# Attention of a sink-and-window layer: float32 probabilities and values in packed column halves instead of float32r high and low parts

## The chip, the cores and the metric

The kernel runs on one core of a Trainium2 chip. The metric is the time of one execution in device microseconds (us); three runs of the kernel before gave 791.02, 791.50 and 791.93, so its time is 791.5 us (median).

## What is computed

Attention over 4 batches, 8 heads, 768 positions, head size 64. Each query sees the last 128 positions up to its own and the first 4 positions (the "sinks"). The output of all heads is the input of a gated feed-forward layer (called MoE in the code) with float64 weights that reach the core as pairs of 32-bit words.

```python
scores = scale * np.matmul(q, k.transpose(0, 1, 3, 2))
keep = is_sink | in_window            # 4 sinks, window of 128
a = np.exp(scores - max); a = a / (sum(a) + 1e-09)
x = np.matmul(a, v)                   # -> 3072 x 512
out = ((x @ w_a) * (x @ w_b)) @ w_out # 512 -> 1536 -> 512
```

## The kernel before, in words

**Chunks.** The rows are worked in eight chunks (CHUNKS, L221): batch, first block of 128 positions, number of blocks nt. The first is (0, 0, 4), the second (0, 4, 2), the other six have nt = 3, three of them from block 0 and three from block 3. While TensorE runs the feed-forward part of chunk c (`moe`, L755), the attention of chunk c + 1 is given out in small steps between its groups of matmuls (`between`, L878). The attention of the first chunk stands alone at the start. The feed-forward part of the last chunk stands alone at the end. In time: about 0 to 52 us the first attention; 52 to 170 the MoE of chunk 0 with the attention of chunk 1 in it, and with the decoding of the weights from words to float32r on VectorE and ScalarE (`weight_bits` to `weight_low`, L324 to L353); then MoE of chunk 1 with the attention of chunk 2 (from block 0), to about 232; then MoE of chunks 2 to 6 with the attention of chunks 3 to 7 (from blocks 0, 3, 3, 0, 3), to about 700.

**The pipeline.** `pipeline` (L713) walks over units (head h, block i). Step k gives out the scores of unit k, then, three units behind, the product with the values of a head whose last unit has been turned (`av`), then the sink products, then the transposes of the unit two behind. This is the order in which the program names the work. The order in which each engine's queue gets it is fixed by a planner before the run, from its own costs and due times; an engine works its queue in order and waits on semaphores.

**Exact attention** (`parts_exact`, L587) serves chunk 0 and the heads 0 to 3 of chunk 1. Scores, probabilities, values and products are float32. The probabilities of a unit are turned by one or two transposes on TensorE (L668) and copied by ScalarE (L669) into a tile that holds two heads. `av` (L671) works on odd heads only: for each block of keys it issues one matmul for the even head into PSUM partitions 0 to 63 (64 columns of the array) and one for the odd head into partitions 64 to 127 (L684). One copy (L687) of 128 partitions brings both heads to `xf`.

**Split attention** (`parts_split`, L456) serves everything else: the heads 4 to 7 of chunk 1 and all heads of chunks 2 to 7, 52 heads in all. Every operand of a matmul is a float32r high part and a float32r rest.
- `prep_v` (L409) loads the values of two heads into an "io" tile (a ring of six), and for each head rounds them (L382 on GpSimd) and takes the rest (L385), so that one 128-column weight tile `vv` holds both parts. In chunk 1 ScalarE (L380) and VectorE (L385) do this.
- The scores are two matmuls (L485, `s`). For late blocks (t >= 2) of batches 1 to 3 the two halves of the window are joined on VectorE by L491 into one square ("joined" units), then follow L493, exp on ScalarE (L495), L497 and L498 on VectorE, and two scalings on ScalarE, L503 for the probabilities `p` and L504 for the sinks `sc`.
- `transposes` of a joined unit: one transpose on TensorE (L524) into a slot of the PSUM tile `t`; ScalarE rounds it (L527); VectorE spreads it by a triangle mask to the two slots of the high part (L528); ScalarE rounds it again into `p` (L530); VectorE subtracts in place (L531) and spreads the rest (L532). Other units: two transposes (L539), a rounding copy (L542), a subtraction (L543).
- `av` of every head multiplies high and low parts (L555): five matmuls of 256 columns where the chunk starts at block 0, seven (five of 256 columns, two of 128) where it starts at block 3, six in chunk 1. The high and low products of the values lie in opposite partition halves, so a copy (L560), an addition (L561) and for nt = 3 another addition (L563) put them together.

Of the kernel before, what the change touches and what calls it, by code (L numbers as in the profile page):

```python
# [7 lines left out]
F32 = mybir.dt.float32  # L8
BF16 = mybir.dt.bfloat16
F32R = mybir.dt.float32r  # L10
# [3 lines left out]
ALU = mybir.AluOpType  # L14
# [3 lines left out]
B, H, S, D = 4, 8, 768, 64  # L18
DM, FF = 512, 1536
P = 128  # L20
# [4 lines left out]
NS = 8  # L25
KB = P + NS
KC = NB * P + (NB - 1) * NS
SW = 2 * P + NS
MB = 4
# [50 lines left out]
def general_path(tc, ident, val, kT, qT, vB, wa, wb, wo, out):  # L80
# [130 lines left out]

UNITS = {3: ((0, 4, "BA"), (1, 2, "AB"), (3, 5, "AB")), 2: ((0, 4, "BA"), (1, 5, "AB"))}
GROUPS = {
    3: ((0, 0, 2, 0), (1, 2, 2, 1), (2, 5, 0, 2), (-1, 4, 1, 0)),
    2: ((0, 0, 2, 0), (1, 5, 1, 1), (-1, 4, 1, 0)),
}


CHUNKS = ((0, 0, 4), (0, 4, 2), (1, 0, 3), (2, 0, 3), (1, 3, 3), (2, 3, 3), (3, 0, 3), (3, 3, 3))  # L221


class Fast:
# [184 lines left out]
    def prep_v(self, b, h, t0, nt):  # L409
        s0, nb, kw, u = self.geometry(b, h, t0, nt)  # L410
        if h % 2 == 0:
            self.vr = self.io([P, 2, MB, D], F32, f"vr{u}")
            self.nc.sync.dma_start(self.vr[:, :, :nb], self.vB[b, h // 2, :, :, s0:s0 + nb])
        vr = self.vr[:, h % 2, :nb]
        vv = self.sp.tile([P, MB, P], F32R, tag="vv", name=f"vv{u}")
        kh, kl = self.halves(h)
        self.round(vv[:, :nb, kh], vr)
        self.rest(vv[:, :nb, kl], vr, vv[:, :nb, kh])
        if h % 4 == 0 and t0 + nt > 2:
            vsr = self.io([P, 2, P], F32, f"vsr{u}")  # L420
# [5 lines left out]
        return vv  # L426

    def attention(self, b, t0, nt, xf, exact=False, alone=False, heads=range(H), bank=None):

# [26 lines left out]
    def parts_split(self, b, t0, nt, xf, alone, heads, bank):  # L456
        nc = self.nc
        tag = f"{b}_{t0}"
        s0 = max(t0 - 1, 0)
        late = [i for i in range(nt) if t0 + i >= 2]  # L460
        units = [(h, i) for h in heads for i in range(nt)]
        tps, preps, state, sc, vss, avs, skt = {}, {}, {}, {}, {}, {}, {}
        banks = self.banks
        joined = late if b else []

        def product(name):
            if bank is None:
                return self.ps.tile([P, 4 * P], F32, tag="av", name=name)
            return self.half_bank(bank, 1, name).rearrange("p c q -> p (c q)")

        def do_prep(h):
            if h in heads:
# [37 lines left out]
        def transposes(h, i):  # L510
            p = state.pop((h, i))
            t = t0 + i
            u = f"{tag}_{h}_{i}"
            n = units.index((h, i))
            if bank is not None:
                tp = self.half_bank(bank, 0, f"t{u}")
            else:
                k = n % len(banks)
                if k not in tps:
                    tps[k] = self.ps.tile([P, 4, P], F32, tag=banks[k], name=f"t{u}")  # L520
                tp = tps[k][:, 2 * (n % 2):2 * (n % 2) + 2, :]
            c1, c2, order = UNITS[nt][i]
            if i in joined:
                nc.tensor.transpose(tp[:, 0, :], p[:, NS:KB], self.ident)  # L524
                hs, ls = (self.pt_split()[:, part, c1:c2 + 1:c2 - c1, :] for part in range(2))
                tri = self.tri if order == "AB" else self.tri[:, ::-1]
# [7 lines left out]
            parts = {"A": p[:, :P], "B": p[:, P + NS:]}  # L534
            if t == 0:
                parts["B"] = p[:, :P]
                order = "B"
            for k, o in enumerate(order):
                nc.tensor.transpose(tp[:, k, :], parts[o], self.ident)  # L539
            n = len(order)  # L540
            hs, ls = (self.pt_split()[:, part, c1:c1 + (n - 1) * (c2 - c1) + 1:c2 - c1, :] for part in range(2))
            nc.scalar.copy(hs, tp[:, :n, :])  # L542
            nc.vector.tensor_tensor(ls, tp[:, :n, :], hs.bitcast(F32), op=ALU.subtract)  # L543

        def av(h):
            vv = preps[h][3]
            ps = product(f"av{tag}_{h}")
            pt = self.pt_split()
            products = []
            for k, sl, ns, c in GROUPS[nt]:  # L550
                if t0 + k >= 0:
                    moving = [pt[:, part, sl:sl + ns, :] for part in range(2)] if ns else [pt[:, :, sl, :]]
                    products += [(t0 + k - s0, m, slice(c * P, (c + (ns or 2)) * P)) for m in moving]
# [3 lines left out]
            x = xf[h // 2]  # L557
            n = nt * P
            mn, mi = self.halves(h)
# [18 lines left out]
        def sinks_av(g, pr):  # L578
            n = len(late) * P
            ps = product(f"sk{tag}_{g}_{pr}")  # L580
            nc.tensor.matmul(ps[:, :n], lhsT=vss[g][:, pr, :], rhs=skt[g][:, :n], start=True, stop=True)
            xs = xf[2 * g + pr][:, late[0] * P:nt * P]
            nc.vector.tensor_tensor(xs, ps[:, :n], xs, op=ALU.add)

        return do_prep, scores, transposes, av, sinks_t, sinks_av

    def parts_exact(self, b, t0, nt, xf, alone, heads, bank):  # L587

        nc = self.nc
        tag = f"{b}_{t0}"  # L590
        s0 = max(t0 - 1, 0)
        nb = t0 + nt - s0
        kw = nb * KB - NS
        late = [i for i in range(nt) if t0 + i >= 2]
        units = [(h, i) for h in heads for i in range(nt)]
        preps, state, sc, vss, pts, skt = {}, {}, {}, {}, {}, {}

        def do_prep(h):
            if h not in heads:
# [54 lines left out]
        def transposes(h, i):  # L654
            p = state.pop((h, i))
            t = t0 + i
            u = f"{tag}_{h}_{i}"
            if not pts:
                pts[0] = self.cp.tile([P, 2, 7, P], F32, tag="pt", name=f"ptx{u}")
# [9 lines left out]
            nc.scalar.copy(pts[0][:, h % 2, k:k + len(parts), :], tp[:, :len(parts), :])  # L669

        def av(h):  # L671
            if h % 2 == 0:
                return
            v = preps[h][2]
            if alone:
                ps = self.ps.tile([P, 4, P], F32, tag="av", name=f"av{tag}_{h}")
            else:
                ps = self.half_bank(bank, 1, f"av{tag}_{h}")
            pin = self.tc.keep_in_program_order
            for blk in range(nb):  # L680
                i0, i1 = max(s0 + blk - t0, 0), min(s0 + blk - t0 + 2, nt)
                sl = 2 * (s0 + blk - t0) + (t0 > 0) + (i0 > s0 + blk - t0)
                for e in range(2):
                    pin(nc.tensor.matmul(ps[e * D:(e + 1) * D, i0:i1, :], lhsT=v[:, e, blk, :],  # L684
                                         rhs=pts[0][:, e, sl:sl + i1 - i0, :], start=blk == 0, stop=blk == nb - 1,
                                         skip_group_check=True))
# [291 lines left out]
```

## Time and profile before

| what | value |
|---|---|
| median of three runs | 791.5 us |
| the profiled execution | 790.77 us |
| its span, first to last instruction | 789.1 us |
| TensorE matmul (PE) busy | 768.3 us, 97% |
| VectorE (DVE) busy | 515.3 us, 65% |
| ScalarE (ACT) busy | 475.5 us, 60% |
| GpSimd (POOL) busy | 290.0 us, 37% |
| mean granted TensorE clock | 0.994 of full speed |

PE is the matmul row and PEld the weight loads, which overlap with it. A matmul's printed duration runs from its start until its result is out. The next one starts before that, so durations of neighbours overlap, and the time that a matmul adds is read from the step between the ends of two neighbours. The chain of waits prints its pieces with just these steps.

### The profile page before, as it was taken

What the parts mean: (1) busy time and instruction counts of PE and PEld (TensorE: products, weight loads), DVE (VectorE), ACT (ScalarE), POOL (GpSimd) and SP (SyncE); (2) the same over time, 40 slices, a digit from 0 to 9 for tenths busy, and PEclk for the clock granted to TensorE, in tenths of its full rate; (3) what the DMA queues carried; (4) which work ended last, traced back from release to release, by engine and by line L of the source; (5) the groups of instructions that cost most, each with busy time, mean ns of one, the idle gap of its engine ahead of it and who ended that gap; (6) DMA issues with size and microseconds to landing.
All of it is one profiled execution on the core that took longest, in us unless ns stands there. A gap on an engine that the chain in (4) does not pass through costs nothing.

```text
span 789.1 us, 13664 instructions
## 1 busy us (share of the span) xinstructions
PE 768.3 (97%) x4293; PEld 673.3 (85%) x4293; DVE 515.3 (65%) x1759; ACT 475.5 (60%) x1479; POOL 290.0 (37%) x400
## 2 busy tenths in 40 slices
PE   8879999999999999999999999999999999999997
PEld 4558777779899999998899889899999988989996
DVE  6878999977774675367763777636765478643321
ACT  5876667747755776466663766547774566644431
POOL 1100000246642664265651756416545466101110
PEclk9989999999999999999999999999999999999999
DMA  8987100142221342412111111113333112005511
GB/s 318 345 310 294 60 18 10 65 142 58 59 68 41 107 132 79 138 31 62 55 48 50 47 43 49 57 41 98 111 119 102 58 52 63 28 30 183 175 55 42
DMA packets 44572, 75.82 MB, mean 96 GB/s; under 512 B 4592, under 2 KB 24016, under 8 KB 44496
## 3 DMA queue, kind: packets, MB, share of 16 engines
q1 hardware_dynamic: 41440, 69.40, 27.0%
q10 hardware_dynamic: 3024, 5.51, 1.9%
q8 instruction: 35, 0.57, 0.3%
q14 instruction: 41, 0.34, 0.1%
q0 software_dynamic: 32, 0.00, 0.0%
HBM read 68.60 MB, written 6.29 MB: 95 GB/s over the span
## 4 chain that ended last, share of the span: by engine, by line
PE 84%; DVE 9%; ACT 3%; DMA 1%; issue 1%; SPq 0%; DVEq 0%; ACTq 0%; POOLq 0%
PE b L769 23%; PE a L769 23%; PE o L778 22%; PE s L485 4%; PE av L555 4%; PE t L524 2%; PE s L631 2%; PE t L539 1%; DVE g L794 1%; DMA kx<-in_kD_dram 1%; PE av L684 1%; DVE w L353 1%; PE t L668 1%; ACT p L495 1%; DVE gl L799 1%
## 5 line engine op out<-in xcount | busy, mean ns | idle before, releaser
L769 PE MATMUL a<-xh,w 128*128 128x384 f32 (+2 forms) x768 | 216.6, 342 | 2.2 <-ACT g L788 1.3
L769 PE MATMUL b<-xh,w 128*128 128x384 f32 (+2 forms) x768 | 214.1, 340 | 0.0
L778 PE MATMUL o<-w,gh 128*128 128x512 f32 x576 | 186.6, 402 | 0.2 <-ACT gh L797 0.2
L769 PEld LDWEIGHTS a<-xh,w 128*128 128x128 f32 x768 | 138.9, 188 | 7.7 <-ACT g L788 1.7
L769 PEld LDWEIGHTS b<-xh,w 128*128 128x128 f32 x768 | 138.8, 188 | 3.7
L799 POOL TENSOR_TENSOR gl<-g,gh 128x384 fp32r<-128x384 f32 x60 | 61.0, 1017 | 188.2 <-ACT gh L797 185.9
L769 PE MATMUL a<-xl,w 128*128 128x384 f32 (+2 forms) x384 | 130.0, 339 | 0.0
L769 PE MATMUL b<-xl,w 128*128 128x384 f32 (+2 forms) x384 | 130.0, 338 | 0.0
L794 DVE TENSOR_TENSOR g<-b,g 128x384 f32<-128x384 f32 (+2 forms) x96 | 53.1, 554 | 108.0 <-PE b L769 97.5
L778 PEld LDWEIGHTS o<-w,gh 128*128 128x128 f32 x576 | 104.2, 189 | 18.5 <-ACT gh L797 0.8
L778 PE MATMUL o<-w,gl 128*128 128x512 f32 x288 | 114.8, 399 | 0.4 <-DVE gl L799 0.4
L788 ACT COPY g<-a 128x384 f32<-128x384 f32 (+2 forms) x96 | 45.5, 474 | 72.6 <-PE a L769 66.7
L797 ACT CAST gh<-g 128x384 fp32r<-128x384 f32 (+2 forms) x96 | 49.1, 512 | 64.1 <-DVE g L794 61.6
L769 PEld LDWEIGHTS a<-xl,w 128*128 128x128 f32 x384 | 72.6, 189 | 2.8 <-issue 0.3
L769 PEld LDWEIGHTS b<-xl,w 128*128 128x128 f32 x384 | 72.5, 189 | 2.2 <-issue 0.3
L495 ACT ACTIVATE p<-p,st 128x264 f32<-128x264 f32 (+1 forms) x152 | 65.4, 430 | 13.6 <-DVE st L493 12.1
L382 POOL TENSOR_SCALAR ks<-kr 64x400 fp32r<-64x400 f32 (+1 forms) x48 | 28.8, 600 | 108.0 <-DVE pt L543 105.9
L778 PEld LDWEIGHTS o<-w,gl 128*128 128x128 f32 x288 | 54.3, 188 | 13.2 <-DVE gl L799 1.7
L382 POOL TENSOR_SCALAR qh<-qr 128x384 fp32r<-128x384 f32 x48 | 25.1, 522 | 103.7 <-PE s L485 96.5
L385 POOL TENSOR_TENSOR ks<-kr,ks 64x400 fp32r<-64x400 f32 (+1 forms) x48 | 57.9, 1205 | 3.9
L503 ACT ACTIVATE p<-p,st 128x128 f32<-128x128 f32 x96 | 38.6, 402 | 24.4 <-DVE st L498 21.8
L555 PE MATMUL av<-pt,vv 128*128 128x256 f32 (+1 forms) x288 | 50.3, 285 | 0.2 <-DVE pt L532 0.2
(153 smaller groups left out, 1388.8 us busy)
## 6 DMA issues: line engine op xcount, KB each, us to landing
qr<-in_qT_dram SPq DMA_DIRECT2D x48, 192.0 KB, 2.4
raw<-in_wa_dram SPq DMA_DIRECT2D x12, 512.0 KB, 6.3
raw<-in_wb_dram SPq DMA_DIRECT2D x12, 512.0 KB, 6.2
raw<-in_wo_dram SPq DMA_DIRECT2D x12, 512.0 KB, 6.0
chk_a<-in_wa_dram SPq DMA_DIRECT2D x24, 256.0 KB, 2.9
chk_b<-in_wb_dram SPq DMA_DIRECT2D x24, 256.0 KB, 2.9
chk_o<-in_wo_dram SPq DMA_DIRECT2D x24, 256.0 KB, 2.8
out_dram<-os ACTq DMA_DIRECT2D x21, 256.0 KB, 2.1
```

Of the source, the lines that this page charges most:

```text
L382: self.nc.gpsimd.tensor_scalar(o, i, 1.0, 1.0, op0=ALU.mult, op1=ALU.mult)
L385: (self.nc.vector if self.no_gpsimd else self.nc.gpsimd).tensor_tensor(o, i, high.bitcast(F32), op=ALU.subtract)
L485: nc.tensor.matmul(ps[:, :w], lhsT=q[:, i * P:(i + 1) * P], rhs=ks[:, c0:c0 + w], start=m == 0, stop=m == 1)
L495: nc.scalar.activation(p[:, :w], p[:, :w], AF.Exp, bias=st[:, 0:1], scale=-1.0, accum_out=st[:, 1:2])
L503: nc.scalar.mul(p[:, NS:KB], p[:, NS:KB], st[:, 3:4])
L555: nc.tensor.matmul(ps[:, cols], lhsT=vv[:, blk, :], rhs=m, start=n == 0, stop=n == len(products) - 1, skip_group_check=True)
L769: nc.tensor.matmul(ps[:, :n], lhsT=w[:, ksl], rhs=x[:, :n], start=kk == 0 and i == 0, stop=kk == NK - 1 and i == 2)
L778: nc.tensor.matmul(outs[i], lhsT=g[:, sl], rhs=w, start=j == 0 and k == 0, stop=j == NJ - 1 and k == 2)
L788: nc.scalar.copy(g[:, :n], pa[:, :n])
L794: nc.vector.tensor_tensor(g[:, :n], pb[:, :n], g[:, :n], op=ALU.mult)
L797: nc.scalar.copy(gh[:, :n], g[:, :n])
L799: e.tensor_tensor(gl[:, :n], g[:, :n], gh[:, :n].bitcast(F32), op=ALU.subtract)
```

## The change

All attention keeps probabilities and values in float32 and uses the product in column halves of the exact attention, for odd heads only, into one PSUM tile. A new function `values` holds that product, for both kinds of attention; it goes through the blocks of keys from the last to the first, and in each takes the odd head first. In split attention, scores, the feed-forward part and the sink products stay as they are. The values of two heads go from memory straight into a "vv" tile (a ring of two). L380, L382 and L385 are gone for the values. Of a joined unit the transpose and one masked multiplication remain; of the others the transposes and the copy. L560, L561 and L563 become one copy of 128 partitions for two heads.

```diff
-    def pt_split(self):
+    def turned(self):
...
-            self.pt = self.cp.tile([P, 2, 7, P], F32R, tag="pt", name="pt")
+            self.pt = self.cp.tile([P, 2, 7, P], F32, name="pt")
...
     def prep_v(self, b, h, t0, nt):
...
-            self.vr = self.io([P, 2, MB, D], F32, f"vr{u}")
-            self.nc.sync.dma_start(self.vr[:, :, :nb], self.vB[b, h // 2, :, :, s0:s0 + nb])
-        vr = self.vr[:, h % 2, :nb]
-        vv = self.sp.tile([P, MB, P], F32R, tag="vv", name=f"vv{u}")
-        kh, kl = self.halves(h)
-        self.round(vv[:, :nb, kh], vr)
-        self.rest(vv[:, :nb, kl], vr, vv[:, :nb, kh])
+            self.v = self.sp.tile([P, 2, MB, D], F32, tag="vv", name=f"v{u}")
+            self.nc.sync.dma_start(self.v[:, :, :nb], self.vB[b, h // 2, :, :, s0:s0 + nb])
...
+    def values(self, ps, v, t0, nt):
+        s0 = max(t0 - 1, 0)
+        nb = t0 + nt - s0
+        pt = self.turned()
+        for blk in reversed(range(nb)):
+            i = s0 + blk - t0
+            i0, i1 = max(i, 0), min(i + 2, nt)
+            sl = 2 * i + (t0 > 0) + (i < 0)
+            for e in (1, 0):
+                self.tc.keep_in_program_order(self.nc.tensor.matmul(
+                    ps[e * D:(e + 1) * D, i0:i1, :], lhsT=v[:, e, blk, :], rhs=pt[:, e, sl:sl + i1 - i0, :],
+                    start=blk == nb - 1, stop=blk == 0, skip_group_check=True))
...
             if i in joined:
                 nc.tensor.transpose(tp[:, 0, :], p[:, NS:KB], self.ident)
-                nc.scalar.copy(tp[:, 1, :].bitcast(F32R), tp[:, 0, :])
-                nc.vector.tensor_tensor(hs, tp[:, 1:2, :].broadcast_to([P, 2, P]), tri, op=ALU.mult)
-                hj = p[:, NS:KB].bitcast(F32R)
-                nc.scalar.copy(hj, tp[:, 0, :])
-                nc.vector.tensor_tensor(tp[:, 0, :], tp[:, 0, :], hj.bitcast(F32), op=ALU.subtract)
-                nc.vector.tensor_tensor(ls, tp[:, 0:1, :].broadcast_to([P, 2, P]), tri, op=ALU.mult)
+                nc.vector.tensor_tensor(pt[:, k:k + 2, :], tp[:, 0:1, :].broadcast_to([P, 2, P]), self.tri,
+                                        op=ALU.mult)
                 return
...
-            nc.scalar.copy(hs, tp[:, :n, :])
-            nc.vector.tensor_tensor(ls, tp[:, :n, :], hs.bitcast(F32), op=ALU.subtract)
+            nc.scalar.copy(pt[:, k:k + len(parts), :], tp[:, :len(parts), :])

         def av(h):
...
-            for n, (blk, m, cols) in enumerate(products):
-                nc.tensor.matmul(ps[:, cols], lhsT=vv[:, blk, :], rhs=m,
-                                 start=n == 0, stop=n == len(products) - 1, skip_group_check=True)
...
-            nc.scalar.copy(x[mn, :n], ps[mi, :n])
-            nc.vector.tensor_tensor(x[mn, :n], ps[mn, :n], x[mn, :n], op=ALU.add)
-            if nt > 2:
-                nc.vector.tensor_tensor(x[mn, 2 * P:], ps[mn, 3 * P:], x[mn, 2 * P:], op=ALU.add)
+            if h % 2 == 0:
+                return
+            ps = product(f"av{tag}_{h}")
+            self.values(ps, preps[h][3], t0, nt)
+            nc.scalar.copy(xf[h // 2][:, :nt * P].rearrange("p (c q) -> p c q", q=P), ps[:, :nt, :])
```

In `parts_exact` the same `turned` tile and the same `values` take the place of its own (the loop over blocks went from the first to the last there, the even head first).

## Rows read from the trace of the kernel before

**Rows 1.** The page: busy time of the engines over the whole span, and the chain of work that ended last, by engine.

```profile
PE 768.3 (97%) x4293; PEld 673.3 (85%) x4293; DVE 515.3 (65%) x1759; ACT 475.5 (60%) x1479; POOL 290.0 (37%) x400
PE 84%; DVE 9%; ACT 3%; DMA 1%; issue 1%; SPq 0%; DVEq 0%; ACTq 0%; POOLq 0%
```

**Rows 2.** Four rows on three stages: the busy time of DVE from 104 to 180 us (stretch, its length, DVE busy and instructions, granted clock, DMA share, GB/s), and the chain of waits by line of the stretches 104 to 180 us, 256 to 330 us and 330 to 427 us, in this order.

```profile
104.00:180.00 76.00, 67.81 (x150) 1.00 0.19 61
by line: PE a L769 14.0%; PE o L778 13.6%; PE b L769 13.3%; DVE w L353 8.4%; DVE wf L343 6.2%; DVE wf L336 6.1%; PE s L485 3.6%; DVE gl L799 3.6%; DVE xl L751 3.6%; issue 3.4%; DVE g L794 3.4%; DVE wf L334 3.1%; DVE pt L543 2.2%; DVE p L493
by line: PE o L778 28.4%; PE b L769 28.3%; PE a L769 25.3%; PE av L555 6.8%; PE s L485 5.7%; PE t L539 3.7%; PE t L524 1.1%; PE sk L581 0.6%; PE skt L570 0.3%; issue 0.0%
by line: PE b L769 25.9%; PE a L769 24.4%; PE o L778 22.9%; PE s L485 5.5%; PE av L555 4.8%; PE t L524 4.1%; DVE g L794 2.3%; DVE pt L532 1.3%; issue 1.2%; ACT gh L797 1.1%; ACT xf L560 1.0%; PE sk L581 0.9%; DVE pt L528 0.9%; PE skt L570 0
```

**Rows 3.** Groups of instructions by line over the whole span: line, engine, operation, tiles, count | busy us, mean ns of one | idle time of the engine just before them and what ended it.

```profile
L531 DVE TENSOR_TENSOR t<-t,p 128x128 f32<-128x128 f32 x96 | 28.5, 297 | 8.8 <-ACT p L530 6.9
L532 DVE TENSOR_TENSOR pt<-t,tri 128x256 fp32r<-128x256 f32 x96 | 40.5, 422 | 1.5
L561 DVE TENSOR_TENSOR xf<-av,xf 64x384 f32<-64x384 f32 x48 | 26.6, 555 | 24.3 <-ACT xf L560 23.3
L527 ACT CAST t<-t 128x128 fp32r<-128x128 f32 x96 | 24.4, 254 | 18.8 <-PE t L524 18.4
L530 ACT CAST p<-t 128x128 fp32r<-128x128 f32 x96 | 25.1, 261 | 16.9 <-DVE pt L528 15.2
L385 POOL TENSOR_TENSOR vv<-vr,vv 128x192 fp32r<-128x192 f32 (+1 forms) x48 | 32.7, 681 | 3.1
```

**Rows 4.** The product with the values before (L555). The first row is from the chain of waits in a stage from block 0: start, time added, piece, number of matmuls. The next two are the timeline of PE in a stage from block 3: start, time until the last result is out, matmuls. The last three are from the chain of waits of another head of that stage.

```profile
255.88 0.60 PE av L555 x5
...
366.24 0.28 PE L485 MATMUL s<-ks,ql 128*128 128x264 f32 x1
366.36 0.93 PE L555 MATMUL av<-pt,vv 128*128 128x256 f32 x7
...
346.94 0.24 PE av L555 x2
348.40 0.15 PE av L555
349.54 0.41 PE av L555 x4
```

**Rows 5.** The product in column halves (L684) of the exact heads, amid the MoE matmuls of chunk 0. The first four rows are the chain of waits from 93.5 to 97 us, the fifth that of the stretch inside the group alone; the sixth gives the weight loads of such groups (minimum, median, maximum ns, then first and last start). One product of the program shows as two matmuls here, since it is full float32.

```profile
93.29 0.93 PE o L778 x4
94.22 0.45 PE s L631 x2
94.66 1.02 PE t L684 x12
95.68 0.90 PE a L769 x3
...
94.92 0.65 PE t L684 x8
...
L684 PEld LDWEIGHTS t<-ptx,vx x24: 133/137/137, 94.6 to 116.0; 128*64 128x64 f32 x24
```

**Rows 6.** Groups by line again (columns as in rows 3): the transposes of joined units, the products before, the turned sinks and the sink product of chunk 1. The idle time of PEld is that before a weight load, that of PE before a matmul.

```profile
L524 PEld LDWEIGHTS t<-ident,p 128*128 128x128 f32 x96 | 13.4, 140 | 10.7 <-issue 6.3 <-ACT sc L504 3.3 <-ACT g L788 0.5
L524 PE MATMUL t<-ident,p 128*128 128x128 f32 x96 | 27.5, 287 | 2.1 <-DVE pt L532 1.9
L555 PEld LDWEIGHTS av<-pt,vv 128*128 128x128 f32 x288 | 41.4, 189 | 5.2 <-DVE pt L532 1.9 <-issue 1.1
L555 PE MATMUL av<-pt,vv 128*128 128x256 f32 (+1 forms) x288 | 50.3, 285 | 0.2 <-DVE pt L532 0.2
L570 PEld LDWEIGHTS skt<-ident,sc 128*32 128x32 f32 x26 | 2.3, 95 | 2.4 <-PE av L555 1.1 <-PE o L778 0.8 <-issue 0.4
L581 PE MATMUL t<-sct,vs 128*128 128x256 f32 x2 | 0.7, 374 | 1.6 <-DVE xf L561 1.6
L581 PEld LDWEIGHTS t<-sct,vs 128*128 128x128 f32 x2 | 0.4, 186 | 2.3 <-ACT raw L335 2.0 <-DVE xf L583 0.3
```

**Rows 7.** The timeline of a few us in a stage from block 3, all engines (start, us, engine, line; in brackets the idle time before it and what ended it).

```profile
361.56 0.42 DVE L532 TENSOR_TENSOR pt<-t,tri 128x256 fp32r<-128x256 f32 x1
...
362.10 0.14 PEld L524 LDWEIGHTS t<-ident,p 128*128 128x128 f32 x1 [0.75 <-issue]
...
362.13 0.30 PE L524 MATMUL t<-ident,p 128*128 128x128 f32 x1 [0.47 <-DVE pt L532]
...
363.21 0.27 ACT L530 CAST p<-t 128x128 fp32r<-128x128 f32 x1
...
363.61 0.40 ACT L503 ACTIVATE p<-p,st 128x128 f32<-128x128 f32 x1
...
364.38 0.14 PEld L524 LDWEIGHTS t<-ident,p 128*128 128x128 f32 x1 [0.29 <-ACT sc L504]
```

**Rows 8.** The first attention, alone. Two pieces of PE's timeline and one between them; the load of the next values on the queue of SyncE; the wait for a load of keys in the chain of waits.

```profile
24.11 0.65 PE L684 MATMUL av<-ptx,vx 128*64 128x256 f32 x4
24.69 0.44 PE L668 MATMUL t<-ident,p 128*128 128x128 f32 x2
25.06 1.40 PE L684 MATMUL av<-ptx,vx 128*64 128x256 f32 x12
...
26.49 0.55 SPq L613 DMA_DIRECT2D vx<-in_vB_dram  x1
...
32.17 7.69 DMA kx<-in_kD_dram
```

More of the change, by code (lines that the diff above doesn't have):

```diff
@@ L461, in parts_split @@
         units = [(h, i) for h in heads for i in range(nt)]
-        tps, preps, state, sc, vss, avs, skt = {}, {}, {}, {}, {}, {}, {}
+        tps, preps, state, sc, vss, skt = {}, {}, {}, {}, {}, {}
         banks = self.banks
@@ L467, in product @@
             if bank is None:
-                return self.ps.tile([P, 4 * P], F32, tag="av", name=name)
-            return self.half_bank(bank, 1, name).rearrange("p c q -> p (c q)")
+                return self.ps.tile([P, 4, P], F32, tag="av", name=name)
+            return self.half_bank(bank, 1, name)
         def do_prep(h):
@@ L521, in transposes @@
                 tp = tps[k][:, 2 * (n % 2):2 * (n % 2) + 2, :]
-            c1, c2, order = UNITS[nt][i]
+            k = max(2 * i - (t0 == 0), 0)
+            pt = self.turned()[:, h % 2]
             if i in joined:
                 nc.tensor.transpose(tp[:, 0, :], p[:, NS:KB], self.ident)
-                hs, ls = (self.pt_split()[:, part, c1:c2 + 1:c2 - c1, :] for part in range(2))
-                tri = self.tri if order == "AB" else self.tri[:, ::-1]
-                nc.scalar.copy(tp[:, 1, :].bitcast(F32R), tp[:, 0, :])
-                nc.vector.tensor_tensor(hs, tp[:, 1:2, :].broadcast_to([P, 2, P]), tri, op=ALU.mult)
-                hj = p[:, NS:KB].bitcast(F32R)
-                nc.scalar.copy(hj, tp[:, 0, :])
-                nc.vector.tensor_tensor(tp[:, 0, :], tp[:, 0, :], hj.bitcast(F32), op=ALU.subtract)
-                nc.vector.tensor_tensor(ls, tp[:, 0:1, :].broadcast_to([P, 2, P]), tri, op=ALU.mult)
-                return
@@ L534, in transposes @@
[L534 to L541, printed above, removed]
-            nc.scalar.copy(hs, tp[:, :n, :])
-            nc.vector.tensor_tensor(ls, tp[:, :n, :], hs.bitcast(F32), op=ALU.subtract)
+                nc.vector.tensor_tensor(pt[:, k:k + 2, :], tp[:, 0:1, :].broadcast_to([P, 2, P]), self.tri,
+                                        op=ALU.mult)
@@ L545, in av @@
+                return
+            parts = [p[:, :P]] if t == 0 else [p[:, :P], p[:, P + NS:]]
+            for m, part in enumerate(parts):
+                nc.tensor.transpose(tp[:, m, :], part, self.ident)
+            nc.scalar.copy(pt[:, k:k + len(parts), :], tp[:, :len(parts), :])
         def av(h):
-            vv = preps[h][3]
+            if h % 2 == 0:
+                return
             ps = product(f"av{tag}_{h}")
[L548 to L553, printed above, removed]
@@ L580, in sinks_av @@
             ps = product(f"sk{tag}_{g}_{pr}")
-            nc.tensor.matmul(ps[:, :n], lhsT=vss[g][:, pr, :], rhs=skt[g][:, :n], start=True, stop=True)
-            xs = xf[2 * g + pr][:, late[0] * P:nt * P]
-            nc.vector.tensor_tensor(xs, ps[:, :n], xs, op=ALU.add)
+            ps = ps[:, :len(late), :]
+            nc.tensor.matmul(ps, lhsT=vss[g][:, pr, :], rhs=skt[g][:, :n], start=True, stop=True)
+            xs = xf[2 * g + pr][:, late[0] * P:nt * P].rearrange("p (c q) -> p c q", q=P)
+            nc.vector.tensor_tensor(xs, ps, xs, op=ALU.add)
         return do_prep, scores, transposes, av, sinks_t, sinks_av
@@ L595, in parts_exact @@
         units = [(h, i) for h in heads for i in range(nt)]
-        preps, state, sc, vss, pts, skt = {}, {}, {}, {}, {}, {}
+        preps, state, sc, vss, skt = {}, {}, {}, {}, {}
         def do_prep(h):
@@ L657, in transposes @@
             u = f"{tag}_{h}_{i}"
-            if not pts:
-                pts[0] = self.cp.tile([P, 2, 7, P], F32, tag="pt", name=f"ptx{u}")
             n = units.index((h, i))
@@ L668, in transposes @@
                 nc.tensor.transpose(tp[:, m, :], part, self.ident)
-            nc.scalar.copy(pts[0][:, h % 2, k:k + len(parts), :], tp[:, :len(parts), :])
+            nc.scalar.copy(self.turned()[:, h % 2, k:k + len(parts), :], tp[:, :len(parts), :])
         def av(h):
@@ L678, in av @@
                 ps = self.half_bank(bank, 1, f"av{tag}_{h}")
[L679 to L686, printed above, removed]
+            self.values(ps, v, t0, nt)
             nc.scalar.copy(xf[h // 2][:, :nt * P].rearrange("p (c q) -> p c q", q=P), ps[:, :nt, :])
```

10 lines of the change are left out of this document (1 added, 9 removed).

## The prediction

> **What bounds the kernel now.** I read the page first: busy times and the chain that ended last [rows 1]. PE is busy 97% of the span and carries 84% of the chain; DVE carries 9%, ACT 3%. So work taken from DVE, ACT or POOL is worth only the time that PE loses to them, and what the change does to PE's own stream counts in full. Next I read the chain stage by stage [rows 2]. From 256 to 330 us (attention from block 0) the chain is PE alone, with no time under issue: nothing but PE's stream can change this stage. From 330 to 427 us (from block 3, every unit joined) about a tenth lies on DVE, ACT and issue, and L532, L528 and L560 of the attention are among it. From 104 to 180 us DVE is busy 67.8 of 76 us, and the decoding of weights (L353, L343, L336, L334) has 23.8% of the chain: that stage is in part DVE's. These three kinds of stage get different answers.
>
> **The sum** is made against the profiled execution, 790.8 us (span 789.1 and 1.7 around it); the median of the runs is 791.5, so 0.7 is added at the end.
>
> *1. The product on PE.* Before, a head costs 0.60 us where the chunk starts at block 0 (five matmuls of 256 columns, 0.47 ns a column) and, where it starts at block 3, from 366.24 + 0.28 = 366.52, the end of the matmul ahead, to 366.36 + 0.93 = 367.29: 0.77 us [rows 4]. For chunk 1 (1024 columns) I take 0.6. So 24 x 0.60 + 24 x 0.77 + 4 x 0.6 = 35.3 us, without waits.
>
> After, one group serves two heads. The nearest rows are L684's [rows 5]. Inside a group, eight matmuls add 0.65 us. They are half of a block of 128 columns, a block of 256 and half of another 128, so 384 columns for both heads: 1.69 ns a column. A single full-width float32 product, L631, takes 0.45 us for 264 columns: 1.70 ns. So two heads in two halves cost what one product costs: the halves run at once. A whole group of 512 columns adds 1.02 us. 512 x 1.69 = 0.87, so 0.15 is paid on entering. The three MoE matmuls after it add 0.90, against 0.93 for four before it: three should take 0.70, so 0.20 is paid on leaving. A group costs 0.35 us plus 1.69 ns a column: 640 columns (block 0) 1.43 us, 768 (block 3) 1.65, 512 (chunk 1) 1.22. Hence 12 x 1.43 + 12 x 1.65 + 2 x 1.22 = 39.4 us, **+4.1**. Alone this makes the kernel slower. Bounds: without entry and exit 30.3 us (-5.0); each time that a group is cut in two it pays another 0.35.
>
> Against this speaks a rule of the Trainium skill, "TensorE: Matmul & The Clock Gate", Part 3: a weight load overlaps with running matmuls only where the row groups differ; in column halves they don't. By that rule the sum would be some 28 us higher (below). The rows say otherwise: loads of 0.137 us, at an added time that is the streaming rate alone [rows 5].
>
> *2. Waits before the products.* The weight loads of L555 find PEld idle 5.2 us in all; idle time before the matmuls themselves is 0.2 [rows 6]. The real loss lies between, since a gap in the loads is partly covered by a running matmul. For one stall both ends are seen: L524 at 362.1 has 0.75 on PEld and 0.47 on PE [rows 7]. I take two thirds of the PEld figure: 3.4 us. They end on L532, the last step of the high and low chain, which vanishes: **-3.3**.
>
> *3. Waits before L524.* 10.7 us on PEld, 2.1 on PE [rows 6]; two thirds are 7.1. Rows 7 show why they go. A transpose waits for a place in the tile `t` until L532 of an earlier unit has read it; between that unit's transpose and L532 stand L527, L528, L530 and L531, and only one multiplication like L532 (0.42 us) is left of it. The next transpose waits for its own probabilities: L503 starts at 363.61 behind L530, and that is gone. I let three quarters go: **-5.3** (bounds 0 and -10.7). Late next are L503 and L504 themselves, after L491 to L498, which all stay.
>
> *4. Sinks.* The sink product of chunk 1 waits 1.6 to 2.3 us for L561 and ACT; the turned sinks 2.4 on PEld [rows 6]. L561 goes, ACT is freer: **-2** (0 to -4.7).
>
> *5. The stage of the weights, 104 to 180 us.* Eight L543, four L561 and four L385 leave DVE, about 6.5 us at some 0.4 each, by the durations of the like-sized L532 and the larger L561 [rows 3]. PE's loss there outside of 2 to 4 is small: **-2.5** (0 to -6.5).
>
> *6. The first attention.* With the last block and the odd head first, no part of the product can start before the last unit is turned. Now four of sixteen matmuls run ahead of that unit's transposes [rows 8]. So the group ends about 0.5 us later, and the load of values at 26.49 waits for it. Behind it on SP's queue are weight loads and the keys whose landing the chain awaits for 7.69 us [rows 8]: **+0.5** (0 to +1.5). Later value loads wait for a "vv" tile where they took an io tile before; it is free a step earlier than they are needed, so I count nothing. Without that cover the keys and queries behind them on SP would be late, and the scores with them.
>
> *7. New waits and cuts.* The first product needs the copy or multiplication of the last unit; some groups will wait or be cut: **+2** (0 to +9).
>
> At nothing: what leaves DVE (L531, L532, L561), ACT (L527, L530) and POOL (L385) beyond this [rows 3], well over 100 us on DVE. PE's stream hides it; where that stream no longer covered it, it would have been in the chain of 256 to 330 us, and it is not [rows 2].
>
> Sum: +4.1 - 3.3 - 5.3 - 2 - 2.5 + 0.5 + 2 = -6.5. From 790.8 that gives 784.3, against the median **785.0 us**.
>
> **The rivals.**
> - *The groups are cut* (slower). The planner may put MoE matmuls between the pieces; then each cut pays entry and exit again. For it: before, products are found in pieces of 2, 1 and 4 [rows 4], and 4 and 12 around two transposes [rows 8]. Against it: those pieces waited for different units, while now the first matmul waits for the last unit and the rest is ready; both groups of chunk 1 are whole. One more cut in each of 26 groups is 26 x 0.35 = 9.1, of which 1.4 is in step 7: 785.0 + 7.7 = 792.7. Two cuts: 801.8. It decides from about 24 cuts on. Chance 0.13.
> - *The waits stay* (no change). The queue's order is fixed from the planner's costs; if it moves the transposes ahead by as much as the chain shrinks, PE waits as before. Then steps 3 to 5 and 7 are 0: +4.1 - 3.3 + 0.5 = +1.3, 792.8; with a third of them gone (-3.3), 789.5; around 791. Chance 0.11.
> - *All waits go*, and DVE's stage gains its whole 6.5: +4.1 - 5.2 - 8 - 4 - 6.5 + 0.5 = -19, 772.4; half way to it from the forecast is 779. Chance 0.12 for below 780.
> - *The halves don't hide their weight loads.* As a mechanism here: a group of 12 or 16 loads, two at a time, would show 6 to 8 times 0.137 us, about 1 us, in 26 groups 25 to 28 us: about 812. The added times of rows 5 leave no room for it. Chance 0.02. This is the page's rule of step 1.
>
> **How the numbers follow.** The forecast, that PE pays about 4 us for entering and leaving and gets back about 10 in waits, has 0.62; with the larger gain, faster has 0.74, and part of "the waits stay" lies below 789.9, which makes 0.76. A difference of 0.2% (1.6 us) is about what a measurement of this kernel can tell from none; within it 0.10; slower 0.14. The range reaches from 778.5, where most of the larger gain is in, to 791.5, where cuts and staying waits begin; left out are about 0.08 below and 0.12 above.
>
> **What would show it.** Right: groups of `values` that add 1.4 and 1.65 us in the chain of waits, uncut, with some 0.2 on the matmul after; the idle time before L524's loads down from 10.7 to about 3; DVE's busy time down by more than 100 us with PE's nearly the same; 256 to 330 us a little longer, the stages from block 3 shorter by 2 to 3 us each. Wrong: groups in pieces, PEld idle before the first load of a group, or SP waiting for a "vv" tile with weights or keys behind it.

## The result and the profile after

The kernel after takes **771.5 us** (median of 4, 771.1 to 771.8) against 791.3 of the kernel before on the same chip: ratio 0.975 (95% interval 0.973 to 0.977), 19.8 us faster. The forecast was 785.0 with a range of 778.5 to 791.5: right in sign, short by 13.5 us, and outside its range. The profiled execution after took 771.08 us, its span is 769.4.

The page of after, as in [rows 1]:

```profile
PE 756.9 (98%) x4341; PEld 661.8 (86%) x4341; DVE 396.2 (52%) x1407; ACT 420.7 (55%) x1257; POOL 240.8 (31%) x304
PE 96%; DVE 2%; issue 1%; ACT 0%; DMA 0%; POOLq 0%; DVEq 0%; ACTq 0%
```

DVE lost 119 us of work and PE 11; the chain, which was PE at 84%, is now PE at 96%. The three kinds of stage, as in [rows 2]: first the busy times from 104 to 180 us (after the length PE, PEld, DVE, ACT, POOL, then granted clock, DMA share and GB/s), then the chain by line of that stretch, of a stage from block 0 (245 to 322 us) and of one from block 3 (322 to 414 us):

```profile
104.00:180.00 76.00, 75.86 (x416) 61.89 (x415) 63.13 (x148) 51.28 (x129) 17.61 (x21) 1.00 0.21 69
...
by line: PE o L748 29.4%; PE b L739 26.7%; PE a L739 25.4%; PE s L487 5.5%; PE t L426 4.0%; PE t L533 3.6%; PE t L677 0.8%; issue 0.8%; PE t L560 0.6%; PE t L645 0.6%; ACT p L508 0.5%; PE skt L548 0.4%; DVE p L495 0.4%; PE t L666 0.3%; PE t
...
by line: PE o L748 29.8%; PE b L739 27.2%; PE a L739 26.0%; PE av L426 6.4%; PE s L487 5.5%; PE t L533 3.6%; PE t L527 1.0%; PE skt L548 0.6%; PE sk L560 0.4%
...
by line: PE o L748 27.9%; PE b L739 27.2%; PE a L739 27.2%; PE s L487 6.7%; PE av L426 6.3%; PE t L527 3.2%; PE skt L548 0.9%; PE sk L560 0.8%
```

The decoding of weights has left the chain of the first stretch, where PE is now busy 75.86 of 76 us (73.63 before), though DVE still works 63 of them. In the stage from block 3 no other engine is left in the chain. The groups that answer to [rows 3, 6]:

```profile
L528 DVE TENSOR_TENSOR pt<-t,tri 128x256 f32<-128x256 f32 x96 | 40.2, 419 | 2.8 <-PE t L527 2.1
L527 PE MATMUL t<-ident,p 128*128 128x128 f32 x96 | 26.4, 275 | 0.0
L426 PEld LDWEIGHTS av<-pt,v 128*64 128x64 f32 x336 | 20.3, 136 | 10.0 <-issue 1.8 <-DVE gl L769 0.4
L527 PEld LDWEIGHTS t<-ident,p 128*128 128x128 f32 x96 | 13.4, 140 | 1.2 <-ACT p L497 1.0
L560 PE MATMUL sk<-sct,vs 128*128 128x128 f32 (+1 forms) x24 | 7.0, 292 | 0.2 <-ACT sct L553 0.2
L560 PEld LDWEIGHTS sk<-sct,vs 128*128 128x128 f32 x24 | 4.5, 189 | 0.3 <-ACT sct L553 0.3
L560 PE MATMUL t<-sct,vs 128*128 128x256 f32 x2 | 0.7, 332 | 0.0
```

L527's loads (L524 before) find PEld idle 1.2 us instead of 10.7, its matmuls 0.0 instead of 2.1; the sink product of chunk 1 (last row) waits 0.0 instead of 1.6. The 10.0 us before L426's own loads are no loss that PE shows: its matmuls wait 0.0, and every group adds just what its columns and the 0.15 us of entering make (below). One product as the chain of waits prints it, beside [rows 4, 7] (start, time added, matmuls):

```profile
361.98 0.52 PE b L739 x3
362.50 0.25 PE s L487 x2
362.75 1.45 PE av L426 x16
364.20 0.43 PE skt L548 x3
364.63 0.11 PE t L527
364.74 1.40 PE o L748 x6
```

Sixteen matmuls add 1.45 us, in one piece; all 32 groups of `values` in the trace are whole.

**Where the 20 us are.** From the ends of PE's matmuls in the profiled executions, in us (start: up to the end of the first MoE matmul; MoE 0 and 1: the MoE of chunks 0 and 1; from 0, from 3: the two and the three MoE stages under an attention from block 0 and from block 3; the last MoE is 75.2 in every kernel). The last column is the median less that of the runs of before beside it.

| kernel | start | MoE 0 | MoE 1 | from 0 | from 3 | against before |
|---|---|---|---|---|---|---|
| before | 44.4 | 128.2 | 68.8 | 181.4 | 285.4 | |
| after | 43.3 | 121.3 | 67.3 | 181.2 | 275.4 | -19.8 |
| e1_order | 44.1 | 124.0 | 68.9 | 181.1 | 285.1 | -4.4 |
| e2_forward | 45.8 | 123.6 | 67.4 | 181.2 | 275.4 | -15.6 |
| e3_short_chain | 44.1 | 127.4 | 68.1 | 181.0 | 277.1 | -11.2 |
| e4_long_chain | 43.3 | 121.7 | 69.2 | 181.6 | 278.1 | -14.4 |
| e5_apart | 46.2 | 123.0 | 68.2 | 183.3 | 283.8 | -4.2 |
| e6_load | 44.2 | 124.6 | 67.6 | 181.3 | 275.4 | -14.9 |
| e7_chain_adds | 43.6 | 122.4 | 70.1 | 182.9 | 279.4 | -9.9 |
| e8_adds | 43.9 | 122.3 | 68.1 | 183.1 | 277.4 | -14.0 |
| e9_order_short | 43.6 | 124.4 | 68.2 | 181.0 | 277.1 | -13.3 |
| e10_product_alone | 44.7 | 125.2 | 70.5 | 183.2 | 286.7 | +2.6 |

Ten of the 20 us lie in the stages from block 3, where the forecast looked for them; seven lie in MoE 0 and one in the start.

### The profile page after: what moved, and what is told of

Same layout as the page of the kernel before. It is cut to its first block, busy times and chain, and to the rows that moved or that the text cites. A ratio compares the mean times of both kernels' runs of the same rounds, so it can differ in the third digit from the quotient of the medians.

```text
span 769.4 us, 13051 instructions
## 1 busy us (share of the span) xinstructions
PE 756.9 (98%) x4341; PEld 661.8 (86%) x4341; DVE 396.2 (52%) x1407; ACT 420.7 (55%) x1257; POOL 240.8 (31%) x304
## 4 chain that ended last, share of the span: by engine, by line
PE 96%; DVE 2%; issue 1%; ACT 0%; DMA 0%; POOLq 0%; DVEq 0%; ACTq 0%
PE a L739 26%; PE o L748 26%; PE b L739 26%; PE av L426 5%; PE s L487 5%; PE s L610 2%; PE t L527 1%; PE t L533 1%; PE t L645 1%; DVE p L617 1%; PE t L426 1%; PE skt L548 1%; PE sk L560 0%; DMA nw_raw<-in_nw_dram 0%; DVE p L624 0%
## 5 line engine op out<-in xcount | busy, mean ns | idle before, releaser
L758 ACT COPY g<-a 128x384 f32<-128x384 f32 (+2 forms) x96 | 45.3, 472 | 74.7 <-PE a L739 70.1
L499 DVE TENSOR_SCALAR st<-st 128x1 f32<-128x1 f32 x152 | 23.2, 153 | 69.0 <-ACT p L497 68.7
```

Of the source, the lines that this page charges most:

```text
L758: nc.scalar.copy(g[:, :n], pa[:, :n])
```

## The experiments

The theory after the result was that the order of the product's blocks frees the start, and the shorter chain the stages from block 3; the rival was that the engines' smaller load does both.

**The order alone, in the exact product of before.**

```diff
-            for blk in range(nb):
+            for blk in reversed(range(nb)):
...
-                for e in range(2):
+                for e in (1, 0):
...
```

> The kernel before with one part of the change: the exact product (chunks 0 and 1) goes from the last block to the first, odd head first; all else as before. Theory of the start: of the 19.8 us, 4.6 are gained in the first 60 us (the first run of twelve MoE matmuls of the second column block starts at 59.2 before and 54.6 after), and they come from this order alone, since it leaves the groups uncut and lets the planner place what follows otherwise: about 786.7 us. Rival, that the start gains by the work that leaves DVE and ACT in chunk 1: within 0.5 us of the kernel before, 791.3.

Measured 787.1 us (785.8 to 787.7), ratio 0.995 (0.993 to 0.996). Two `for` lines (and the marks of the first and last block that go with them), no work removed, -4.4 us.

**The order turned back in after** (the same two lines of `values`, the other way).

> The changed kernel with the product's order turned back: first block to last, even head first. The queues show that the groups of the split heads stay whole and only chunk 0's are cut, into 3, 2, 2 and 1 pieces. Theory of the start: the 4.6 us of the start go back, 776 us, and from 60 us on everything lasts as long as in the changed kernel. Rival, that the start gains by the work that leaves DVE and ACT: 771.5 to 772.5.

Measured 775.9 us (774.3 to 776.3), ratio 0.980 (0.978 to 0.981): 4.2 us of after's gain go, all of them in the start and MoE 0. How it works shows in the chain of waits of before, 42 to 60 us:

```profile
42.91 0.63 ACT w L348
...
43.59 1.22 PE a L769 x2
...
47.57 0.43 PE t L668 x2
48.00 2.31 PE av L684 x16
...
57.61 1.03 ACT w L348
58.64 0.49 ACT g L788
...
59.18 3.02 PE a L769 x12
```

and of after:

```profile
46.64 1.66 PE av L426 x16
...
54.63 3.02 PE a L739 x12
```

In before two MoE matmuls stand in PE's queue ahead of the last two pairs of score matmuls, and PE waits 0.98 us for a decoded weight (`w`); the product ends at 50.31. In after they stand one pair later and find their weight there, and the product ends at 48.30. The load of the next values on SyncE's queue follows the product, and raw weights follow that load; before and after:

```profile
50.35 0.55 SPq L613 DMA_DIRECT2D vx<-in_vB_dram  x1
52.81 0.41 SPq L311 DMA_DIRECT2D raw<-in_wa_dram  x1
...
48.35 0.55 SPq L592 DMA_DIRECT2D vx<-in_vB_dram  x1
50.48 0.41 SPq L304 DMA_DIRECT2D raw<-in_wa_dram  x1
```

These are 2.0 and 2.3 us earlier, but no load is what PE waits for in before when the run of twelve MoE matmuls stands ready. That is `g` (L788), ScalarE's copy of the block of MoE columns ahead. ScalarE does it last, behind a weight's rounding (L348); in after it comes first, right behind the matmuls that it copies. ScalarE's timeline, before and after:

```profile
57.61 1.03 ACT L348 CAST w<-wf 128x1024 fp32r<-128x1024 f32 x1
58.55 0.58 ACT L788 COPY g<-a 128x512 f32<-128x512 f32 x1
...
53.99 0.59 ACT L758 COPY g<-a 128x512 f32<-128x512 f32 x1 [0.94 <-PE a L739]
54.47 1.05 ACT L341 CAST w<-wf 128x1024 fp32r<-128x1024 f32 x1
```

So the run of twelve begins at 54.63 instead of 59.18. PE from 42 to 52 and 52 to 64 us (length, PE busy first, then PEld, DVE, ACT, POOL; granted clock), before:

```profile
42.00:52.00 10.00, 8.63 (x36) 5.37 (x37) 7.11 (x20) 6.57 (x14) 0.77 (x2) 0.66 0.82 310
52.00:64.00 12.00, 10.74 (x46) 7.97 (x46) 10.92 (x19) 10.06 (x20) 0.00 (x0) 1.00 0.82 299
```

and after:

```profile
42.00:52.00 10.00, 10.00 (x45) 6.21 (x45) 8.33 (x20) 7.69 (x16) 0.78 (x2) 0.79 0.90 330
52.00:64.00 12.00, 12.00 (x54) 9.59 (x53) 11.03 (x18) 10.04 (x17) 0.00 (x0) 1.00 1.01 389
```

In after all 22 us are filled. The granted clock stands at its lower level (half of full speed) for some of this stretch in both, and in before part of that falls on the product (2.31 us instead of 1.66). What this costs shows in e3_short_chain, whose PE queue is the one of before in this stretch, matmul by matmul, with a granted clock of 0.83 instead of 0.66 from 42 to 52 us:

```profile
47.51 1.71 PE av L680 x16
...
58.10 3.03 PE a L765 x12
```

Its product ends at 49.22 and its twelve begin at 58.10. So some 1.1 of the 4.5 us between before and after are the clock in this execution of before; the rest, some 3.5, is the order. In the four kernels with the first block in front (before, e2_forward, e3_short_chain, e10_product_alone) the twelve begin at 58.10 to 59.94; in the seven with the last block in front and the heads in turn at 54.27 to 55.20, in e1_order, with the order alone, at 54.33. Why the planner puts the two MoE matmuls and `g` where it does with one order and not with the other was not tried.

**The short chain alone, in before.**

```diff
+            self.nc.gpsimd.memset(self.pt[:, 1].bitcast(F32), 0.0)
...
-                nc.scalar.copy(tp[:, 1, :].bitcast(F32R), tp[:, 0, :])
-                nc.vector.tensor_tensor(hs, tp[:, 1:2, :].broadcast_to([P, 2, P]), tri, op=ALU.mult)
...
-                nc.vector.tensor_tensor(ls, tp[:, 0:1, :].broadcast_to([P, 2, P]), tri, op=ALU.mult)
+                nc.vector.tensor_tensor(hs, tp[:, 0:1, :].broadcast_to([P, 2, P]), tri, op=ALU.mult)
```

> The kernel before, but a joined unit ends after its transpose with the one masked multiplication (L527, L530, L531, L532 gone); the low parts of the joined units' probabilities are left out, and the product still runs over their places, so TensorE's product is the old one. Theory of the chain: the three stages from block 3 fall from 95.2 to about 92.5 us each, since the waits before the transposes (2.4 us a stage), the turned sinks and the products go with the chain; the stages from block 0, one joined unit in three, by 0.2 to 0.5; in all 782.5 us. Rival, that these stages gain by the product in column halves (whole groups, half as many): they stay near 95, 791 in all.

Measured 780.3 us (780.1 to 781.7), ratio 0.987 (0.985 to 0.988): -11.2, of which 8.3 in the stages from block 3. In the profiled executions, 790.77 and 780.24, some 1.1 us of the difference lie at the start and are the clock's, as shown above.

**The long chain put back into after.**

```diff
+                nc.scalar.copy(tp[:, 1, :], tp[:, 0, :])
+                nc.vector.tensor_tensor(pt[:, k:k + 2, :], tp[:, 1:2, :].broadcast_to([P, 2, P]), self.tri,
+                                        op=ALU.mult)
+                hj = p[:, NS:KB]
+                nc.scalar.copy(hj, tp[:, 0, :])
+                nc.vector.tensor_tensor(tp[:, 0, :], tp[:, 0, :], hj, op=ALU.max)
```

> The changed kernel with the long chain put back for joined units, as copies that change no value: ACT copy, masked multiplication, ACT copy, DVE maximum in place, masked multiplication again, each on what the one before it left. The product is the new one. Theory of the chain: the stages from block 3 rise from 91.8 to about 94.3 us, 779 us in all. Rival, that the product brings the gain: 771.5 to 772.

Measured 777.1 us (776.2 to 777.9), ratio 0.982 (0.981 to 0.983): 5.4 us come back, half of the 11.2 that the same chain was worth in before. In the stages from block 3 it is 2.7 instead of 8.3. That is between the theory and its rival. So what the chain is worth depends on what stands beside it; this run alone doesn't tell whether that is the product, its order or its way out of PSUM.

**The halves apart**: all blocks of the odd head, then all of the even one.

```diff
-        for blk in reversed(range(nb)):
-            for e in (1, 0):
+        for e in (1, 0):
+            for blk in reversed(range(nb)):
```

> The changed kernel with the two heads of a product apart: all blocks of the odd head, then all of the even head, the same matmuls in another order. Theory that the two column halves run at once: a group now streams each head by itself, 1.69 ns a column more: 18,900 columns in the groups amid MoE matmuls give 32 us, chunk 0's 3,600 up to 6 more, so 804 to 810 us; a group of 768 columns goes from 1.45 to 2.75 us. Rival, that the halves gain nothing from their order: 771 to 773 us.

Measured 787.3 us (786.5 to 787.8), ratio 0.995 (0.993 to 0.996). The same group in the chain of waits, which counts fourteen of its sixteen matmuls:

```profile
369.79 0.25 PE s L487 x2
370.04 2.15 PE av L426 x14
372.19 0.43 PE skt L548 x3
```

2.15 us instead of 1.45. Two heads wholly one after the other would add 0.15 + 2 x 1.30 = 2.75 (768 columns at 1.69 ns each), two at once 1.45. So the halves do run at once, as step 1 read from [rows 5], but here only for part of the time: of the even head's eight matmuls the first starts at 370.68, with the odd head's fifth of eight (370.67). The expectation missed the size because it left no room for that. What keeps the even head from starting earlier was not tried.

**Chunk 1's old load put back** (value-keeping instructions on DVE and ACT).

```diff
...
+            if bank is not None:
+                nc.vector.tensor_tensor(pk, tp[:, :len(parts), :], pk, op=ALU.max)
...
+                nc.scalar.copy(v, v)
+                nc.vector.tensor_tensor(v, v, v, op=ALU.max)
...
+                for e in range(2):
+                    nc.vector.tensor_tensor(x, ps[:, :nt, :], x, op=ALU.max)
```

> The changed kernel with the old load of chunk 1's split heads put back on DVE and ACT, as operations that change no value (per unit a DVE pass over the turned tile, per head a DVE and an ACT pass over the values, per pair two DVE passes over the product). Theory of the weights' stage: about 6 us more DVE work while DVE decodes weights costs 1 to 3 us in the stage of the first MoE, 773 to 774 us. Rival, that this stage gained by the start and the sink product alone: 771.5.

Measured 776.5 us (775.6 to 777.7), ratio 0.982 (0.980 to 0.983). MoE 0 is 3.3 longer and the start 0.9: more than the theory said. Load on DVE and ACT does cost time in this stage, but PE loses it at other places than in before: from 60 to 172 us it waits 1.7 us for `gh` (ACT), 1.0 for a weight (ACT) and 0.4 for `gl` (DVE), where in before it waits 1.6 for the sinks, 0.4 for `gl` and 0.2 for `gh`, and in after for none of these.

**The long chain and the old way out of PSUM**, three instructions for each head instead of one copy for two (the lines of the long chain are as above).

```diff
-            nc.scalar.copy(xf[h // 2][:, :nt * P].rearrange("p (c q) -> p c q", q=P), ps[:, :nt, :])
+            x = xf[h // 2][:, :nt * P].rearrange("p (c q) -> p c q", q=P)
+            for e in range(2):
+                r = slice(e * D, (e + 1) * D)
+                nc.scalar.copy(x[r], ps[r, :nt, :])
+                nc.vector.tensor_tensor(x[r], ps[r, :nt, :], x[r], op=ALU.max)
+                if nt > 2:
+                    nc.vector.tensor_tensor(x[r, 2:], ps[r, 2:nt, :], x[r, 2:], op=ALU.max)
```

> The changed kernel with the long chain and, for each half of a product, the old way out of PSUM: ACT copy, DVE pass, for three blocks another DVE pass (values unchanged). The long chain alone had cost 0.9 us in a stage from block 3, while the short chain in the kernel before had gained 2.8. Theory of the sum: the waits before the transposes come when chain and additions together fill DVE and ACT, so here a stage from block 3 takes 94 to 95 us and the whole 781 to 783. Rival, that the rest of the gain is the new product's: as with the long chain alone, 92.6 a stage, 777 to 778.

Measured 781.5 us (780.3 to 782.5), ratio 0.988 (0.986 to 0.990). The total fits and the place does not: the stages from block 3 are 93.1 each, not 94 to 95.

**The old way out alone** (the same edit without the chain).

> The changed kernel with the old way out of PSUM alone, the chain short. Theory of the sum: hidden, a stage from block 3 takes 91.8 to 92.2, the whole 771.5 to 773. Rival, that the additions alone make transposes wait: 93 a stage, 775 to 776.

Measured 777.4 us (776.6 to 777.7), ratio 0.982 (0.981 to 0.983): the old way out costs 5.8 us here, more than either expectation. A stage from block 3 takes 92.5, and the transposes that the rival named do not wait (PEld is idle 1.2 us before them, as in after). The sink products do (L566, L560 of after):

```profile
L566 PE MATMUL sk<-sct,vs 128*128 128x128 f32 (+1 forms) x24 | 7.9, 329 | 1.2 <-DVE xf L547 0.7
L566 PEld LDWEIGHTS sk<-sct,vs 128*128 128x128 f32 x24 | 4.5, 187 | 5.0 <-issue 3.5 <-ACT pt L534 1.1
...
L566 PE MATMUL t<-sct,vs 128*128 128x256 f32 x2 | 0.7, 333 | 1.2 <-DVE xf L568 1.2
```

The sink product takes the one place in PSUM that the product leaves (both have the tag `av`). Two heads now leave it together, six instructions in a row, right ahead of the sink product: PEld is idle 5.0 us where after shows 0.3. Counted from end to end of neighbouring matmuls, the sink products add 8.8 us here, 3.9 in after and 6.5 in before, where each head leaves by itself. So most of the 5.8 us are this wait, and it is larger than the one that before had.

**The order and the short chain, in before**: is what is left to after the product itself?

> The kernel before with two edits that were each tried alone: the exact product goes from the last block to the first with the odd head first (alone 787.1, 4.3 off), and of the joined units' chain one masked multiplication is left (alone 780.3, 11.1 off; the low parts are zeros in it). The product of high and low parts, its way out of PSUM and the rounding of the values stay. If the order, which works at the start and in the stage of the weights, and the chain, which works in the stages from block 3, do not meet, their gains add: 776 us, and the 4.5 us left to the kernel after (771.5) are the product, its way out and the values' preparation. Rival: the order is worth less once the chain is short, because both take load from the same stretch of the stage of the weights (chunk 1's heads 4 to 7 carry no joined units, which speaks against it): 778 to 780. Other rival: the product and its way out are worth nothing beside these two: 772 to 773.

Measured 777.4 us (777.0 to 777.9), ratio 0.984 (0.982 to 0.985): -13.3, where the two alone make -4.4 and -11.2. That is 2.3 us less than their sum, between the theory and its first rival; each of the three differences is uncertain by about 1 us, so they meet a little at most.

**The product alone**: after with the long chain, the old way out and the old order.

> The kernel after with all three other edits turned back in their load: the joined units' chain as value-keeping copies, three instructions out of PSUM for each head pair half, and the product from the first block to the last, the even head first. What is left of the change is the product in column halves itself and the values that go straight into their tile. If effects add: 781.5 (long chain and old way out) + 4.4 (order) = 785.9 us, so the product with the values alone gains 5.5 on the kernel before, though by the sum of the prediction it should cost 0.8 with its waits taken in. Rival: the order only mattered because the chain and the adds were off the engines; with their load back it is worth under 1: 781 to 782.5. Other rival: the product is worth nothing by itself: 790 to 792.

Measured 793.4 us (792.5 to 794.9), ratio 1.0034 (1.0023 to 1.0046): **slower than before**, by 2.6 us. All three expectations failed, the first rival by the most (11 us), the last by the least (1.4): the effects don't add. The chain of waits in a stage from block 3 (next to the 1.45 us of after):

```profile
353.63 0.25 PE s L487 x2
353.88 0.36 PE av L426 x2
354.24 0.26 PE t L527
354.50 1.01 PE av L426 x7
355.52 1.41 PE b L751 x7
356.93 0.79 PE av L426 x5
357.72 0.26 PE t L527
```

The mechanism of the prediction's slower rival is here. With the first block in front, two matmuls are ready before the last units are turned; the planner sets them ahead, and the group comes in three pieces, 0.36 + 1.01 + 0.79 = 2.16 us. Half of the groups in these stages are cut so. With the order turned and the rest the same (e7_chain_adds) none is, and 12.5 us go: 7.3 of them in these stages, 3.9 in the start and MoE 0. The order alone doesn't cut, though: in e2_forward, first block in front with the short chain and the single copy, all these groups are whole and the stages from block 3 take 275.4 us, as in after.

Nor is all of the 2.6 us the product's. The sink products add 9.7 us here, 6.5 in before, since two heads leave PSUM together; and the subtraction of the units that are not joined (L543) was not put back.

**Two ladders**, each step the difference of two medians, each taken against the runs of before beside it, and uncertain by 1 to 2 us. "Product and values" takes in that L543 is gone, and that the old way out then serves two heads at once:

| from before to after | step | step | step | step |
|---|---|---|---|---|
| product last but one | order -4.4 | short chain -8.9 | product and values -0.7 | way out -5.8 |
| product first | product and values +2.6 | order -12.5 | short chain -4.1 | way out -5.8 |

The -0.7 can't be told from nothing.

## Why the prediction fell short

**Steps 1 and 2, the product with its waits: +0.8 forecast, -0.8 found.** Most of step 1's sizes hold. Groups of 640, 768 and 512 columns add 1.23, 1.45 and 1.02 us, as 1.69 ns a column and 0.15 on entering make them. The price of leaving was taken too high: 0.20 for every group, from the one row with MoE matmuls behind it. But of the 28 groups behind the start 25 have a transpose behind them, and that pays 0.11 (sinks, 13 times) or 0.15 (probabilities, 12 times). Matmul by matmul the old product with its waits cost 38.4 us; the new one adds 34.2 and about 3.4 on leaving. By the Trainium skill's rule on weight loads ("TensorE: Matmul & The Clock Gate", Part 3), loads overlap with running matmuls only where the row groups differ; the prediction estimated from it about 1 us more for each group. The trace does not agree: loads of 0.136 us are hidden here too.

**Steps 3 and 4, waits before L524 and sinks: -7.3 forecast, some -12.6 found.** The transposes of the split units added 29.5 us before and 22.9 after: 6.6 less, 8.4 if the leaving price of the twelve groups ahead of one (0.15 each) is charged to the product. "Three quarters go" was too careful, and two thirds of the PEld figure too: in after next to nothing of that idle time is left. The sinks fell by 4.2 instead of 2, by the same count. The forecast costed L561 only where the trace of before showed a wait on it; e8_adds shows a wait that the new product itself would have made, and the single copy prevents.

**Step 5, the stage of the weights: -2.5 forecast, about -2 left over.** With the sinks and the first 15 us taken out, some 2 us of MoE 0's 6.9 are left. That they come from the smaller load is not shown: e6_load makes the stage 3.3 us longer, but by other waits than those of before.

**Step 6, the first attention: +0.5 forecast, -4.5 found, some 1.1 of it the clock. This is the step that failed most.** The delay that it named is there. The second product begins only when its last unit is turned, and the load of values that went out at 26.49 goes out at 27.14 in after; but the keys further behind it, at 32.17 before, do not go out later:

```profile
27.14 0.55 SPq L592 DMA_DIRECT2D vx<-in_vB_dram  x1
...
32.14 1.01 SPq L588 DMA_DIRECT2D kx<-in_kD_dram  x1
```

So the forecast's 0.5 us got lost on the way, and at the end of the first attention the sign was wrong. The step was reasoned from one change, that the product can no longer start early, with the rest of every queue's order held fixed; but the order is planned anew. The last product ended 2.0 us earlier (0.9 of it when the clock is taken out), and `g` came ahead of the weight's rounding. No bound below zero had been given, although nothing excluded a gain.

**Step 7, cuts and new waits: +2 forecast, 0 found.** All groups are whole and their matmuls wait 0.0. The argument against the cutting rival, that the first matmul now waits for the last unit while the rest is ready, holds where the long chain and the old way out are put back: e10_product_alone has cuts and e7_chain_adds none. Without these the groups in the MoE stages stay whole in either order (e2_forward).

Together: -5.0 (step 6), -3.1 (step 3), -2.2 (step 4), -2.0 (step 7), -1.6 (steps 1 and 2) and +0.5 (step 5) are 13.4 of the 13.5 us. The time found is that of the rival "all waits go" (772.4), and that is in part luck: its terms for the waits fit, but it counted 6.5 us for the stage of the weights, where some 2 are found, and +0.5 for the start, where 4.5 were gained. Nearly all terms of the forecast erred to the same side, and they are not independent: removing the chain is worth 8.9 us with the old product and 4.1 with the new one, the order 4.2 to 12.5. That the long chain and a cut or waiting product each keep up one and the same stretch of waiting would explain this; it was not shown by itself.

What stays open is how the planner comes to its orders, and how far order and load share the gain of MoE 0: e6_load and e2_forward each bring back part of the start.

## What to carry to other kernels

Where a queue's order is planned from data dependences, the order in which a product walks its blocks is a lever of its own: try it with what is ready last in front. It was worth 4.4 us here with nothing else changed, and 12.5 where, with a long chain ahead of it, the product otherwise came in pieces. Price a stall with several causes as one thing: halves of it assigned to single causes are either counted twice or missed. And when an order is planned anew, give the forecast a bound on both sides of zero. A product that costs TensorE more per column paid here only together with the other edits: with the old way out of PSUM it made no difference that could be told from nothing (-0.7 us), and with the long chain and the old order as well it was slower (+2.6).

## What the runs showed of the hardware

- Matmuls in opposite column halves run at once when they alternate (768 columns for two heads: 1.45 us); in two runs of eight only in part (2.15 us). Each half's order of blocks is the same in both; only the interleaving differs.
- Entering such a group costs 0.15 us net (its first matmul adds 0.25 us, where its columns make 0.11). Leaving it costs the next matmul 0.11 us (a transpose of the sinks), 0.15 (a transpose of probabilities) or 0.20 (a MoE matmul).
